# Attention of the last three batches: row sums on VectorE and a transposing DMA, in a fused attention and bilinear feed-forward kernel

## The chip, the cores and the metric

The kernel runs on one core of a Trainium2 chip. The metric is the device time of one execution in microseconds (us), and the median of several runs is compared. A core has TensorE (PE in the profile; its weight loads are PEld), VectorE (DVE), ScalarE (ACT), GpSimd (POOL) and SyncE (SP), each with its own instruction stream, and 16 DMA engines. L12 is line 12 of the kernel.

## The reference

A linear attention without softmax, normalised by the root of the mean square along each head, is followed by a feed-forward layer that multiplies two projections.

```python
# q, k, v: (batch 8, heads 8, seq 576, head_dim 64), float32
def _attn_ref(q, k, v, g_norm):
    kv = np.einsum('bhsd,bhse->bhde', k, v)
    out = np.einsum('bhsd,bhde->bhse', q, kv)
    rms = np.sqrt(np.mean(out * out, axis=-1, keepdims=True) + 1e-06)
    return (out / rms * g_norm)

# x: the attention's output as (4608 tokens, 512); w_a, w_b: (512, 1536); w_out: (1536, 512)
def _moe_ref(x, w_a, w_b, w_out):
    a = x @ w_a
    b = x @ w_b
    return (a * b @ w_out)
```

## The kernel before

**Work in two kinds.** The attention goes batch by batch (576 tokens each), the feed-forward block by block (512 tokens each, nine blocks). Both share all engines, so a batch's attention is woven between the matmuls of the blocks before the one that needs its tokens. The feed-forward takes x d-major: a column for each token, the 512 features (head pairs p = 0 to 3 of 128 features) on the partitions. These columns lie in `xp`, a ring of four batches (`R = 4 * S`), and `xcols(p, t0, n)` names n of them.

**The feed-forward.** Block 0 is plain (`std_block`, `o_std`). Blocks 1 to 8 use a Strassen form with seven products in place of eight (`wino_block` for the projections, L742; `o_unit` for the output, L911). Its sums are VectorE's work: L711 forms differences of x columns, L761 combines a PSUM bank with an evicted copy, L796 multiplies the two projections, L896 forms sums of the products, L949 combines outputs. ScalarE evicts banks (L415, L943).

**Attention of batches 2 to 7 (`late_batch`).** `load_node` has POOL issue the loads of k and v and a copy of q in bf16 to a DRAM scratch `scr`, and SP a transposing DMA that brings q d-major into `qT` (L587). Before its first load each later batch's node copies one element of the previous batch's qT to `gate_t` (L563), which makes POOL wait until that transpose has landed. `kv_mm` (L533) forms the eight 64 x 64 products, two heads to a 128 x 128 diagonal block `kvd`. Then `slices` does, for each of four head pairs and two halves of 288 tokens:

1. TensorE, L348 (`x_mm`): x = kvd times qT, d-major in PSUM;
2. ScalarE, L358 (`sq_op`): its square, in bf16;
3. TensorE, L362 (`s_mm`): a product with `ones` (blocks of 1/64), which puts a head's mean square on all of its partitions;
4. ScalarE, L366 (`rs_op`): the reciprocal root;
5. VectorE, L371 (`xt_op`): x times `g_col` times that root, to `xp` in fp16.

Batches 0 and 1 (`early_batch`) take another way to kvd and q and then the same `slices`.

**What sets the order.** `Plan` is a list scheduler that runs when the kernel is built. Every step is a node with an engine, an estimated duration, a priority (a time in us), its dependencies and the buffers that it takes and frees. `Plan.order` goes through the engines, gives each the node that can start first, the lowest priority among those ready, and emits the instructions in that order. On the chip each engine runs its stream in that order and waits on semaphores. A dependency written `(node, 8.0)` is taken by the planner as met 8.0 us after that node's end: with this it reckons with a DMA's landing. `at_win[b]` (L1025) is the window of priorities of batch b's attention, worked out from the planned starts `st` of the blocks: about 137 to 152, 171 to 184 and 206 to 216 us for batches 5, 6 and 7. The priority of the load of batch b is the window's start of batch b - 1. `RQ` and `RS` are rings of PSUM banks 5 to 7 with two held at once each, `RX` and `RY` the same over banks 0 to 3.

The estimates of durations:

```python
    def mm_us(n, cols):
        return n * (cols / 2400 + 0.0025)

    def act_us(n, bias=False):
        return (0.155 if bias else 0.06) + n / 1200

    def dve_us(n):
        return (n + 65) / 960
```

Of the kernel before, what the change touches and what calls it, by code (L numbers as in the profile page):

```python
# [8 lines left out]
FP32 = mybir.dt.float32  # L9
BF16 = mybir.dt.bfloat16  # L10
FP16 = mybir.dt.float16
AF = mybir.ActivationFunctionType  # L12
ALU = mybir.AluOpType
# [122 lines left out]
def kernel(  # L136
# [11 lines left out]
    nc = tc.nc  # L148

    B, H, S, D = q.shape  # L150
    d_model = H * D
# [30 lines left out]
    EH = d_model // 2  # L182

    const = ctx.enter_context(tc.tile_pool(name="const", bufs=1))
    scr_pool = ctx.enter_context(tc.tile_pool(name="scr", bufs=B, space=bass.MemoryType.DRAM))
    psum = ctx.enter_context(tc.tile_pool(name="psum", bufs=1, space=bass.MemoryType.PSUM))
    ctx.enter_context(tc.manual_schedule())

    def sb(name, shape, dt):
        return const.tile(shape, dt, name=name)  # L190
# [15 lines left out]
    as_t = sb("as", [128, 4, NJ, 256], FP16)  # L206
    b_ts = [sb(f"c{i}", [128, 4, 2, NMAX], FP16) for i in range(2)]
    u_t = sb("u", [128, 6, 2, NMAX], FP32)
    sq_ts = [sb(f"sq{i}", [128, HF], BF16) for i in range(3)]
    rs_ts = [sb(f"rs{i}", [128, HF], FP32) for i in range(3)]  # L210
    o_ts = [sb(f"o_sb{i}", [128, 4, d_model], FP32) for i in range(2)]

# [95 lines left out]
    def xcols(p, t0, n):  # L308
        return xp[p // 2][:, p % 2, t0 % R : t0 % R + n]
# [94 lines left out]
# [5 lines that stand above are left out]
# [7 lines left out]
        ]  # L416

    T0 = 20.0
    plan = Plan({"PE": 5.7, "DVE": 3.3, "ACT": 2.7, "SP": 5.0, "POOL": 22.5, "V": 0.0})
    PB, PA, PO = Pool(banks[0:4]), Pool(banks[5:8]), Pool(banks[4:5])  # L420
    RX, RY, RO = Ring(PB, 2), Ring(PB, 2), Ring(PO)
    RQ, RS = Ring(PA, 2), Ring(PA, 2)
    RU, RB, RAB = Ring([u_t[:, i] for i in range(6)]), Ring(b_ts), Ring(ab_ts)
    RT, RAS = Ring([T_t[:, i] for i in range(5)]), Ring([as_t[:, i] for i in range(4)])
    RSQ, RRS, ROS = Ring(sq_ts), Ring(rs_ts), Ring(o_ts)
    RK, RV, RQT, RKD = Ring(k_ts), Ring(v_ts), Ring(qT_ts), Ring(kvd)
    normed = {}
# [14 lines left out]
    def slices(at, win, extra):  # L442
        w0, w1 = win
        for i in range(2 * NP):
            p, h = divmod(i, 2)
            pr = w0 + (w1 - w0) * i / (2 * NP)
            x, s = ((Buf(RX), Buf(RY)) if at.b == 0 and i % 3 == 1 else (Buf(RQ), Buf(RS)))
            sq, rs = Buf(RSQ), Buf(RRS)
            ta = at.b * S + h * HF
            war = [  # L450
                n
                for j, (a, b) in enumerate(blocks_of)
                if a < ta - R + HF and b > ta - R
                for n in readers.get(j, ())
            ]
            n1 = plan.add(
                "PE", mm_us(1, HF), pr,
                lambda p=p, h=h, x=x: at.x_mm(p, h, x.tile), extra(p), [x], at.qt,
            )
            n2 = plan.add(  # L460
                "ACT", act_us(HF), pr, lambda p=p, h=h, b=sq: at.sq_op(p, h, b.tile), [n1], [sq]
            )
            n3 = plan.add(
                "PE", mm_us(1, HF), pr,
                lambda p=p, h=h, s=s: at.s_mm(p, h, s.tile), [n2], [s], [sq],
            )
            s_done[at.b] = n3
            n4 = plan.add(
                "ACT", act_us(HF, True), pr,
                lambda p=p, h=h, b=rs: at.rs_op(p, h, b.tile), [n3], [rs], [s],  # L470
            )
            normed[at.b, p, h] = plan.add(
                "DVE", dve_us(HF) + 0.06, pr,
                lambda p=p, h=h: at.xt_op(p, h), [n4] + war + ([g_n] if at.b == 0 else []), (), [x, rs],
            )

    def early_batch(b, win):
# [35 lines left out]
            done[p] = [n2, n4]  # L513
        slices(at, win, lambda p: done[p])

    def late_batch(b, load, win):
        at = Attn(b)
        w0, w1 = win
        kb, vb, qb = load["k"], load["v"], load["q"]
        kd = Buf(RKD)  # L520
        at.qt = [qb, kd]

        def view(t):
            return t[:, 0 : H * (NCH + 1) * D].rearrange("p (h c d) -> p h c d", h=H, d=D)

        s = Buf(RS)

        def kv_mm():
            kv_ps = s.tile[:].rearrange("p (a e) -> p a e", a=NP)
            for c in range(NCH + 1):  # L530
                for p in range(NP):
                    hs = slice(2 * p, 2 * p + 2)
                    nc.tensor.matmul(  # L533
                        kv_ps[:, p, :],
                        lhsT=kb.tile[:, c, hs, :],
                        rhs=view(vb.tile)[:, hs, c, :],
                        start=(c == 0 and p == 0),
                        stop=(c == NCH and p == NP - 1),
                    )

        n = plan.add(
            "PE", 1.15, w0, kv_mm, [(load["n"], load["kv_us"]), plan.at(w0 - 3)], [s, kd], [kb, vb]
        )

        def kv_out():
            kv_ps = s.tile[:].rearrange("p (a e) -> p a e", a=NP)
            at.kvd = kd.tile
            nc.scalar.copy(at.kvd[0:D, :, 0:D], kv_ps[0:D, :, 0:D])
            nc.scalar.copy(at.kvd[D:, :, D:], kv_ps[D:, :, D:])
            for p in range(NP):  # L550
                at.q[p] = qb.tile[:, p, :]

        m = plan.add("ACT", 0.75, w0, kv_out, [n], (), [s])
        slices(at, (w0 + 0.12 * (w1 - w0), w1), lambda p: [m, (load["qn"], 8.0)])


    def load_node(b, prio, dep):
        ld = {"k": Buf(RK), "v": Buf(RV), "q": Buf(RQT)}
        scr = scr_pool.tile([NP, S, 2, D], BF16, name="scr", tag="scr")

        def issue():
            if dep is not None:
                nc.gpsimd.tensor_copy(gate_t, dep["q"].tile[0:1, 0, 0:1])  # L563
            qv = q[b].rearrange("(p hl) s d -> hl s p d", hl=2)
            for hl in range(2):
                nc.gpsimd.dma_start(  # L566
                    out=scr[:, :, hl, :].rearrange("p s d -> s p d"), in_=qv[hl]
                )
            kt = ld["k"].tile
            ks = k[b, :, 0:SA, :].rearrange("h (sp c) d -> sp h c d", c=NCH)  # L570
            for c in range(NCH):
                nc.gpsimd.dma_start(out=kt[:, c], in_=ks[:, :, c, :])  # L572
            nc.gpsimd.dma_start(out=kt[0:SB, NCH], in_=k[b, :, SA:S, :].rearrange("h sp d -> sp h d"))
            for n, src in (("v", v),):
                t = ld[n].tile[:, 0 : H * (NCH + 1) * D].rearrange(
                    "p (h c d) -> p h c d", h=H, d=D
                )
                nc.gpsimd.dma_start(
                    out=t[:, :, 0:NCH, :],
                    in_=src[b, :, 0:SA, :].rearrange("h (sp c) d -> sp h c d", c=NCH),  # L580
                )
                nc.gpsimd.dma_start(
                    out=t[0:SB, :, NCH, :], in_=src[b, :, SA:S, :].rearrange("h sp d -> sp h d")
                )

        def transpose():
            nc.sync.dma_start_transpose(  # L587
                out=ld["q"].tile[:].rearrange("p a s -> p (a s)"),
                in_=scr[:].rearrange("a s h d -> (a s) (h d)"),
            )  # L590

        issue_us, q_us, ld["kv_us"] = (15.4, 4.3, 13.0) if dep is None else (9.0, 5.0 if b == 3 else 1.8, 13.0)

        ld["n"] = plan.add(
            "POOL", issue_us, prio, issue, [(dep["qn"], 8.0)] if dep else [], [ld["k"], ld["v"]]
        )
        ld["qn"] = plan.add(
            "SP", 2.5, prio, transpose, [(ld["n"], q_us)], [ld["q"]]
        )
        return ld  # L600
# [422 lines left out]
    for b in range(2, B):  # L1023
        t = b * S / N0
        at_win[b] = (max(53.0, st[int(t) - 1] + (t % 1) * L[int(t) - 1] - 18), st[int(t)] - 22 + (t % 1) * 12)  # L1025
    loads = {2: load_node(2, 22.5, None)}
    wo_n = load_wo(loads[2])
    for b in range(3, B):
        loads[b] = load_node(b, at_win[b - 1][0], loads[b - 1])
    gb = Buf(RQ)  # L1030
    g_in = plan.add(
        "PE", 0.07, 8.5, lambda: nc.tensor.transpose(gb.tile[:, 0:1], g_row, one), [plan.at(6.4)], [gb]
# [10 lines left out]
    for bi in range(1, nb + 1):  # L1043
        o_win = (st[bi] + 1.0, st[bi + 1] - 1.0) if bi < nb else (st[bi] + O_A, st[bi + 1] + O_B)
        if bi == 1:
            o_std(ab, muls, (o_win[0] + 4.0, o_win[1] + 4.0))
            osum = out_sums(st[2] - 10)
        else:
            o_block(bi - 1, ab, muls, osum, o_win, 2, (RO, RY, RY), 1)
        for b in needs[bi]:  # L1050
            late_batch(b, loads[b], at_win[b])
        ab, muls = wino_block(bi, (st[bi], st[bi + 1]), wsum)
    o_block(
        nb, ab, muls, osum, (st[nb + 1], st[nb + 1] + o_us[nb]), NJ // 2,
# [38 lines left out]
```

## Time and profile before

| what | value |
|---|---|
| median of 3 runs | 299.74 us (299.61 to 299.81) |
| the profiled execution | 299.53 us |
| its span, first to last instruction | 297.8 us |
| TensorE busy, share of the span | 290.5 us, 98% |
| VectorE busy | 234.0 us, 79% |
| ScalarE busy | 192.4 us, 65% |
| DMA traffic | 32.72 MB |
| first and last x of the attention written (L371) | at 10.8 and 224.6 us |

The profiled execution is one run, recorded by the hardware profiler. Its span leaves out what lies before the first and after the last instruction, here 1.7 us. A busy time is the union of the recorded durations of an engine's instructions. A matmul's record is longer than the distance to the next matmul's start, because matmuls are pipelined: a 256-column matmul is recorded with 273 ns and the next starts after 109. So TensorE's pace is read from starts.

### The profile page before, as it was taken

How to read it: one execution, taken by the hardware profiler on the slowest of the kernel's cores; microseconds unless marked ns; L12 is line 12 of the kernel's file. 1: busy time of each engine (PE TensorE's matmuls, PEld its weight loads, DVE VectorE, ACT ScalarE, POOL GpSimd, SP SyncE). 2: the span in 40 equal slices, each digit the busy share in tenths (PEclk: the TensorE clock that was granted, in tenths of full speed). 3: DMA queues.
4: the chain of work that ended last, by engine and by line, in shares of the span. 5: the costliest groups of instructions: out<-in, count | busy, mean ns of one | idle time of the engine just before them, and what ended most of it. 6: DMA issues, size and time to landing. Idle time of an engine off the chain costs nothing.

```text
span 297.8 us, 6705 instructions
## 1 busy us (share of the span) xinstructions
PE 290.5 (98%) x2635; PEld 238.9 (80%) x2635; DVE 234.0 (79%) x435; ACT 192.4 (65%) x401; POOL 76.7 (26%) x95
## 2 busy tenths in 40 slices
PE   8999999999899999999999999999999999999993
PEld 3645559865788988889888988889888888888882
DVE  5544879894976998889779977997599859897762
ACT  3847767865588577866787658954996466654521
POOL 8945830940190650380560000000000000000000
PEclk9999999999999999999999999999999999999999
DMA  8999999799999699699999200020004001100043
GB/s 178 199 199 199 194 159 155 119 166 186 202 113 172 94 191 174 42 136 210 136 146 222 74 0 2 36 108 0 2 0 143 1 2 70 73 3 0 34 144 108
DMA packets 98195, 32.72 MB, mean 110 GB/s; under 512 B 74612, under 2 KB 94068, under 8 KB 98164
## 3 DMA queue, kind: packets, MB, share of 16 engines
q0 software_dynamic: 77552, 18.44, 65.3%
q1 hardware_dynamic: 20000, 13.16, 20.3%
q10 hardware_dynamic: 612, 0.71, 0.8%
q8 instruction: 20, 0.33, 0.5%
q14 instruction: 11, 0.09, 0.1%
HBM read 37.75 MB, written 12.98 MB: 170 GB/s over the span
## 4 chain that ended last, share of the span: by engine, by line
PE 71%; DMA 22%; POOL 4%; issue 1%; DVE 1%; ACT 0%; DVEq 0%; SPq 0%; POOLq 0%
PE bk L742 42%; PE bk L911 24%; DMA scr<-in_q_dram 8%; DMA v_t<-in_v_dram 4%; DMA wb_t<-in_moe_w_b_dram 4%; DMA qT<-scr 3%; DMA wa_t<-in_moe_w_a_dram 3%; PE bk L362 2%; PE bk L348 2%; PE bk L533 2%; POOL as L237 1%; POOL so L237 1%; POOL scr L566 1%; DVE o_sb L949 1%; POOL wo_t L609 1%
## 5 line engine op out<-in xcount | busy, mean ns | idle before, releaser
L761 DVE TENSOR_TENSOR c<-bk,u 128x512 f16<-128x512 f32 x144 | 96.6, 685 | 25.2 <-ACT u L415 12.8
L415 ACT COPY u<-bk 128x512 f32<-128x512 f32 x144 | 81.8, 590 | 37.3 <-PE bk L742 33.8
L742 PE MATMUL bk<-xp,wa_t 128*128 128x256 f16 x288 | 54.9, 273 | 0.0
L742 PE MATMUL bk<-xp,wb_t 128*128 128x256 f16 x288 | 54.9, 273 | 0.0
L371 DVE SCALAR_TENSOR_TENSOR xp<-bk,g_col,rs 128x288 f16<-128x288 f32 x64 | 32.4, 511 | 14.3 <-ACT rs L366 14.3
L742 PEld LDWEIGHTS <-wa_t 128*128 128x128 f16 x384 | 37.4, 98 | 5.7
L911 PEld LDWEIGHTS <-abt 128*128 128x128 f16 x384 | 37.4, 98 | 4.7 <-DVE abt L796 0.2
L742 PEld LDWEIGHTS <-wb_t 128*128 128x128 f16 x384 | 37.6, 98 | 4.4
L415 ACT CAST c<-bk 128x512 f16<-128x512 f32 x48 | 28.1, 590 | 17.7 <-PE bk L742 16.9
L911 PE MATMUL bk<-wo_t,abt 128*128 128x256 f16 x288 | 36.8, 273 | 0.0
L742 PE MATMUL bk<-T,sb 128*128 128x256 f16 x192 | 36.6, 273 | 0.0
L742 PE MATMUL bk<-T,sa 128*128 128x256 f16 x192 | 36.6, 273 | 0.0
L366 ACT ACTIVATE rs<-bk,eps_t 128x288 f32<-128x288 f32 x64 | 32.3, 508 | 5.7 <-PE bk L362 5.2
L796 DVE TENSOR_TENSOR abt<-c 128x1024 f16<-128x1024 f16 x48 | 32.9, 686 | 1.8
L742 PEld LDWEIGHTS <-sa 128*128 128x128 f16 x288 | 28.1, 98 | 3.8
L911 PEld LDWEIGHTS <-as 128*128 128x128 f16 x288 | 28.2, 98 | 3.5
L742 PEld LDWEIGHTS <-sb 128*128 128x128 f16 x288 | 28.2, 98 | 3.3
L943 ACT COPY o_sb<-bk 128x512 f32<-128x512 f32 x31 | 18.2, 587 | 15.2 <-PE bk L911 14.8
L358 ACT ACTIVATE sq<-bk 128x288 bf16<-128x288 f32 x64 | 25.5, 414 | 1.3 <-PE bk L348 0.6
L911 PE MATMUL bk<-so,as 128*128 128x256 f16 x192 | 25.5, 273 | 0.0
L572 POOL DMA_DIRECT2D k_t<-in_k_dram x24 | 21.2, 897 | 0.7 <-issue 0.5
L566 POOL DMA_DIRECT2D scr<-in_q_dram x12 | 19.6, 1637 | 2.6 <-issue 1.4
(99 smaller groups left out, 396.5 us busy)
## 6 DMA issues: line engine op xcount, KB each, us to landing
out_dram<-o_sb SPq DMA_DIRECT2D x20, 256.0 KB, 2.3
scr<-in_q_dram POOLq DMA_DIRECT2D x12, 288.0 KB, 8.2
k_t<-in_k_dram POOLq DMA_DIRECT2D x24, 128.0 KB, 8.8
v_t<-in_v_dram POOLq DMA_DIRECT2D x6, 512.0 KB, 10.9
out_dram<-o_sb SPq DMA_DIRECT2D x18, 128.0 KB, 2.4
wa_t<-in_moe_w_a_dram POOLq DMA_DIRECT2D x6, 256.0 KB, 10.7
wb_t<-in_moe_w_b_dram POOLq DMA_DIRECT2D x6, 256.0 KB, 10.9
wo_t<-in_moe_w_out_dram POOLq DMA_DIRECT2D x2, 768.0 KB, 9.4
```

Of the source, the lines that this page charges most:

```text
L237: nc.gpsimd.dma_start(out=t[n][:, hs, :, :], in_=src[b, hs].rearrange("h (sp c) d -> sp h c d", c=EC),)
L358: nc.scalar.activation(sq, self.x_ps[p, h][:, 0:HF], AF.Square)
L366: nc.scalar.activation(rs, self.s_ps[p, h][:, 0:HF], AF.Abs_reciprocal_sqrt, bias=eps_t)
L371: nc.vector.scalar_tensor_tensor(out=xcols(p, self.b * S + h * HF, HF), in0=self.x_ps[p, h][:, 0:HF], scalar=g_col, in1=self.rs[p, h], op0 ...
L415: ("ACT", act_us(n), lambda: nc.scalar.copy(*args())),
L566: nc.gpsimd.dma_start(out=scr[:, :, hl, :].rearrange("p s d -> s p d"), in_=qv[hl])
L572: nc.gpsimd.dma_start(out=kt[:, c], in_=ks[:, :, c, :])
L742: nc.tensor.matmul(ps.tile[:, i * n : (i + 1) * n], lhsT=lhs(w, sm)[:, kc, :], rhs=rhs()[:, kc, :], start=start and i == 0 and kc == 0, st ...
L761: lambda: nc.vector.tensor_add(cs(fi, h), full(ps), u.tile),
L796: nc.vector.tensor_mul(t, c[:, :, :, 0], c[:, :, :, 1])
L911: nc.tensor.matmul(ps.tile[:, sub * EH : (sub + 1) * EH], lhsT=lhs(slice(j, j + 1))[:, 0, sub * 128 : (sub + 1) * 128], rhs=rhs[:, j, :], ...
L943: lambda: nc.scalar.copy(o(fi, h), bank(X, every)), [dep], takes, frees,
```

## The change

For batches 5, 6 and 7 (`TB = 5`) `late_batch` calls `token_tiles` in place of `slices`. It takes the batch's 576 tokens in five tiles of 128 (the last overlaps the fourth and keeps 64). For each, x comes token-major, tokens on the partitions and 512 features in the row, from four matmuls with q as the stationary operand and kvd as the moving one. ScalarE squares the whole tile, VectorE sums each head's 64 squares with a reduce, ScalarE takes eight reciprocal roots for each token, VectorE multiplies x by them into fp16, and SP stores the tile to a DRAM scratch `xs`. After the five stores SP issues four transposing DMAs (`turn`), one for each head pair, from `xs` to the columns in `xp`. VectorE then multiplies these columns by `g_col` in place, in two instructions. The planner takes the transposes as landed `TURN = 9.0` us after their node's end.

The windows of these batches start and end 13 us earlier (`AHEAD`). The load of batch 7 also waits for the turn of batch 5, by one more copy to `gate_t`. The load nodes are made just before their batch's attention instead of all at the start. The planner's estimate for the landing of batch 3's k and v goes from 13 to 16 us. There are two square buffers of 512 columns where there were three of 288.

```diff
@@
-    sq_ts = [sb(f"sq{i}", [128, HF], BF16) for i in range(3)]
+    sq_ts = [sb(f"sq{i}", [128, d_model], BF16) for i in range(2)]
+    ss_t = sb("ss", [128, 3, 2 * H], FP32)
+    xt_t = sb("xt", [128, 2, d_model], FP16)
@@
+    TB, TURN, AHEAD = 5, 9.0, 13.0
@@
+    RSS, RXT = Ring([ss_t[:, i] for i in range(3)]), Ring([xt_t[:, i] for i in range(2)])
@@
+    def token_tiles(at, win, dep):
+        b = at.b
+        w0, w1 = win
+        xs = xscr_pool.tile([NP, S, 128], FP16, name="xs", tag="xs")
+        stored, tiles = [], [(i * 128, 128) for i in range(NCH)] + [(S - 128, SB)]
+        for i, (j0, keep) in enumerate(tiles):
+            pr = w0 + (w1 - w0) * i / len(tiles)
+            X, sq, ss, xt = Buf(RQ), Buf(RSQ), Buf(RSS), Buf(RXT)
+
+            def mm(j0=j0, X=X):
+                for p in range(NP):
+                    nc.tensor.matmul(
+                        X.tile[:, p * 128 : (p + 1) * 128],
+                        lhsT=at.q[p][:, j0 : j0 + 128],
+                        rhs=at.kvd[:, p, :],
...
+            n1 = plan.add("PE", 0.23, pr, mm, dep, [X], at.qt)
+            n2 = plan.add(
+                "ACT", act_us(d_model), pr,
+                lambda X=X, sq=sq: nc.scalar.activation(sq.tile, X.tile[:], AF.Square), [n1], [sq],
+            )
+            n3 = plan.add(
+                "DVE", dve_us(d_model), pr,
+                lambda sq=sq, ss=ss, heads=heads: nc.vector.tensor_reduce(
+                    out=ss.tile[:, 0:H], in_=heads(sq.tile), axis=mybir.AxisListType.X, op=ALU.add
+                ),
+                [n2], [ss], [sq],
+            )
+            n4 = plan.add(
+                "ACT", act_us(H, True), pr,
+                lambda ss=ss: nc.scalar.activation(
+                    ss.tile[:, H:], ss.tile[:, 0:H], AF.Abs_reciprocal_sqrt, bias=eps_t, scale=1.0 / D
+                ),
+                [n3],
+            )
+            n5 = plan.add(
+                "DVE", dve_us(d_model), pr,
+                lambda X=X, ss=ss, xt=xt, heads=heads: nc.vector.tensor_mul(
+                    heads(xt.tile), heads(X.tile[:]), ss.tile[:, H:].unsqueeze(2).to_broadcast([128, H, D])
+                ),
+                [n4], [xt], [X, ss],
+            )
+
+            def save(j0=j0, keep=keep, xt=xt):
+                nc.sync.dma_start(
+                    out=xs[:, j0 + 128 - keep : j0 + 128, :].rearrange("a s e -> s a e"),
+                    in_=xt.tile[128 - keep :].rearrange("p (a e) -> p a e", a=NP),
+                )
+
+            stored.append(plan.add("SP", 0.45, pr, save, [n5], (), [xt]))
...
+        def turn():
+            for p in range(NP):
+                nc.sync.dma_start_transpose(out=xcols(p, b * S, S), in_=xs[p])
+
+        n6 = plan.add("SP", 2.5, w1, turn, stored + war)
+        for i in range(2):
+            xg = xp[i][:, :, b * S % R : b * S % R + S]
+            n7 = plan.add(
+                "DVE", 0.4, w1, lambda xg=xg: nc.vector.tensor_scalar_mul(xg, xg, g_col), [(n6, TURN)]
+            )
...
+        if b >= TB:
+            return token_tiles(at, (w0 + 0.12 * (w1 - w0), w1), [m, (load["qn"], 8.0)])
         slices(at, (w0 + 0.12 * (w1 - w0), w1), lambda p: [m, (load["qn"], 8.0)])
@@ load_node
+            if xt is not None:
+                nc.gpsimd.tensor_copy(gate_t, xcols(NP - 1, (b - 2) * S, 1)[0:1])
...
-        issue_us, q_us, ld["kv_us"] = (15.4, 4.3, 13.0) if dep is None else (9.0, 5.0 if b == 3 else 1.8, 13.0)
+        issue_us, q_us, ld["kv_us"] = (15.4, 4.3, 13.0) if dep is None else (9.0, 5.0 if b == 3 else 1.8, 16.0 if b == 3 else 13.0)
...
-            "POOL", issue_us, prio, issue, [(dep["qn"], 8.0)] if dep else [], [ld["k"], ld["v"]]
+            "POOL", issue_us, prio, issue, ([(dep["qn"], 8.0)] if dep else []) + ([(xt, TURN)] if xt else []), [ld["k"], ld["v"]]
@@
+        if b >= TB:
+            at_win[b] = tuple(x - AHEAD for x in at_win[b])
@@
-            late_batch(b, loads[b], at_win[b])
+            if b > 2:
+                loads[b] = load_node(b, at_win[b - 1][0], loads[b - 1], turned.get(b - 2))
+            turned[b] = late_batch(b, loads[b], at_win[b])
```

More of the change, by code (lines that the diff above doesn't have):

```diff
@@ L184 @@
     const = ctx.enter_context(tc.tile_pool(name="const", bufs=1))
+    xscr_pool = ctx.enter_context(tc.tile_pool(name="xscr", bufs=B, space=bass.MemoryType.DRAM))
     scr_pool = ctx.enter_context(tc.tile_pool(name="scr", bufs=B, space=bass.MemoryType.DRAM))
@@ L460, in slices @@
             n2 = plan.add(
-                "ACT", act_us(HF), pr, lambda p=p, h=h, b=sq: at.sq_op(p, h, b.tile), [n1], [sq]
+                "ACT", act_us(HF), pr, lambda p=p, h=h, b=sq: at.sq_op(p, h, b.tile[:, 0:HF]), [n1], [sq]
             )
@@ L514, in early_batch, with heads @@
         slices(at, win, lambda p: done[p])
+    def token_tiles(at, win, dep):
[12 more added lines that the diff above has]
+                        rhs=at.kvd[:, p, :],
+                        start=(p == 0),
+                        stop=(p == NP - 1),
+                        skip_group_check=True,
+                    )
+            def heads(ap):
+                return ap.rearrange("p (h d) -> p h d", d=D)
+            n1 = plan.add("PE", 0.23, pr, mm, dep, [X], at.qt)
[30 more added lines that the diff above has]
+            stored.append(plan.add("SP", 0.45, pr, save, [n5], (), [xt]))
+        war = [
+            n
+            for j, (u, v) in enumerate(blocks_of)
+            if u < (b + 1) * S - R and v > b * S - R
+            for n in readers.get(j, ())
+        ]
+        def turn():
[6 more added lines that the diff above has]
+                "DVE", 0.4, w1, lambda xg=xg: nc.vector.tensor_scalar_mul(xg, xg, g_col), [(n6, TURN)]
+            )
+            for p in (2 * i, 2 * i + 1):
+                for h in range(2):
+                    normed[b, p, h] = n7
+        return n6
@@ L553, in late_batch, with load_node @@
         m = plan.add("ACT", 0.75, w0, kv_out, [n], (), [s])
+        if b >= TB:
+            return token_tiles(at, (w0 + 0.12 * (w1 - w0), w1), [m, (load["qn"], 8.0)])
         slices(at, (w0 + 0.12 * (w1 - w0), w1), lambda p: [m, (load["qn"], 8.0)])
-    def load_node(b, prio, dep):
+    def load_node(b, prio, dep, xt=None):
         ld = {"k": Buf(RK), "v": Buf(RV), "q": Buf(RQT)}
@@ L1025 @@
         at_win[b] = (max(53.0, st[int(t) - 1] + (t % 1) * L[int(t) - 1] - 18), st[int(t)] - 22 + (t % 1) * 12)
+        if b >= TB:
+            at_win[b] = tuple(x - AHEAD for x in at_win[b])
     loads = {2: load_node(2, 22.5, None)}
     wo_n = load_wo(loads[2])
-    for b in range(3, B):
-        loads[b] = load_node(b, at_win[b - 1][0], loads[b - 1])
+    turned = {}
     gb = Buf(RQ)
```

## The prediction

> **What bounds the kernel now.** I read the busy table first, then the groups by line, then TensorE's timeline, because a busy share of TensorE is modelled and can hide small gaps.
>
> ```profile
> span 297.8 us, 6705 instructions
> PE 290.5 (98%) x2635; PEld 238.9 (80%) x2635; DVE 234.0 (79%) x435; ACT 192.4 (65%) x401; POOL 76.7 (26%) x95
> ```
>
> The reader is to see one engine near the whole span, and VectorE (DVE) next at 79%. The timeline of TensorE (start, duration, instruction) around two of the six k-times-v products tells whether TensorE is really full:
>
> ```profile
> 76.90 1.06 PE L533 MATMUL bk<-v_t,k_t 128*128 128x128 bf16 x16
> 79.15 0.38 PE L533 MATMUL bk<-v_t,k_t 128*128 128x128 bf16 x4 [1.19 <-DMA v_t<-in_v_dram]
> ```
> ```profile
> 138.57 1.28 PE L533 MATMUL bk<-v_t,k_t 128*128 128x128 bf16 x20
> 139.69 0.38 PE L742 MATMUL bk<-xp,wa_t 128*128 128x256 f16 x2
> ```
>
> In the second pair twenty matmuls of 128 columns take 139.69 - 138.57 = 1.12 us from start to the next start: 56 ns each. Matmuls of 256 columns start every 109 ns (the chain has twelve in 1.31 us), and those of 288 every 122 ns: all are columns / 2.4 plus 2.5 ns. I compared every start-to-start distance from 45 to 293 us with that rule: the excess sums to 1.50 us, and 1.35 us of it is the one gap in the first pair, where batch 3's product waits for v. So from 45 us on TensorE is the bound, with no other wait; only its columns, that gap, and new waits can move the end.
>
> The groups that the change touches (busy sum, mean ns), all with 64 instructions, eight for each batch:
>
> ```profile
> L371 DVE SCALAR_TENSOR_TENSOR xp<-bk,g_col,rs 128x288 f16<-128x288 f32 x64 | 32.4, 511 | 14.3 <-ACT rs L366 14.3
> L366 ACT ACTIVATE rs<-bk,eps_t 128x288 f32<-128x288 f32 x64 | 32.3, 508 | 5.7 <-PE bk L362 5.2
> L358 ACT ACTIVATE sq<-bk 128x288 bf16<-128x288 f32 x64 | 25.5, 414 | 1.3 <-PE bk L348 0.6
> ```
>
> and the stretches of one feed-forward block each in which batches 5 to 7 fall (PE, PEld, DVE, ACT, POOL busy):
>
> ```profile
> 105.30:135.80 30.50, 30.50 (x280) 27.12 (x278) 26.90 (x49) 22.16 (x45) 12.41 (x15) 1.00 1.58 141
> 135.80:166.30 30.50, 30.50 (x289) 27.25 (x288) 26.15 (x48) 21.96 (x46) 9.21 (x10) 1.00 1.39 167
> 166.30:196.80 30.50, 30.50 (x289) 27.21 (x288) 25.67 (x48) 21.74 (x46) 0.00 (x0) 1.00 0.11 34
> 196.80:227.30 30.50, 30.50 (x289) 27.23 (x288) 25.21 (x47) 21.74 (x46) 0.00 (x0) 1.00 0.10 30
> ```
>
> VectorE has 3.6 to 5.3 us free of each 30.5; ScalarE (ACT) 8.3 or more.
>
> **What the Trainium skill says.** "TensorE: Matmul & The Clock Gate", section "Back-to-back issue gap", gives a sustained 81 ns for a 128-column matmul with its own weights, and 56 ns for an isolated one. The trace has 56 ns over twenty in a row, each with a new weight load, so I take 56 and keep 81 as a bound. "VectorE: DVE Perf Modes", section "The perf-mode tier table", has tensor_reduce at one element a cycle whatever the type, and tensor_scalar on 16-bit SBUF data at four. No row of before shows either. "DMA: Bandwidth & Descriptors", section "Two DMAs through the same engine are not ordered", says that completion order isn't kept in one queue, so the turning transposes must wait for the stores' landing; the q path already shows such a wait (SP on scr, 68.0 us in five waits).
>
> **TensorE, part by part.** For one batch the change removes 8 products with kvd and 8 with ones, 288 columns each: 16 x 0.1225 = 1.96 us. It adds 5 tiles of 4 matmuls of 128 columns: 20 x 0.056 = 1.12 us. Net -0.84 us, three batches -2.52 us; at 81 ns a matmul it would be -0.34 and -1.0. The longer load estimate of batch 3 (16 instead of 13 us) lets the planner place its k-times-v product up to 3 us later, after v has landed at 79.1, with other matmuls in front. I count the whole 1.35 us; the lower end is nothing, if no other matmul is ready then.
>
> **ScalarE.** Removed for a batch: 8 x (0.414 + 0.508) = 7.4 us. Added: 5 squares of 512 elements (the 512-element copy of L415 is 0.590) and 5 reciprocal roots of 8 elements (the one-element warm-up took 0.203), about 4.0 us. It gains 3.4 us, hidden under TensorE: worth nothing by itself.
>
> **VectorE.** Removed: 8 x 0.511 = 4.1 us. Added: 5 reduces of 512 and 5 products of 512 from PSUM, both at L761's 0.685 (one element a cycle as well), 6.9 us, and two multiplications by g over 1152 fp16 elements. At four a cycle 0.46 each, estimated from that page's 693 ns for 2048; at two, from L796's 686 ns for 1024, 0.75. I take 0.46, so 7.8 us against 4.1: +3.7 us a batch, +11.1 in all (+12.8 at most). The four stretches hold 103.9 us; 115.0 must fit in 122.0 - 2.5 = 119.5. That is 96%. It fits, but not in place: each batch's tiles are planned 13 us earlier, into 124 to 139, 158 to 171 and 193 to 203 us, where VectorE already had 89%, 95% and 94%. Taking the old x operations out (0.5 us in each of the first two) and 6.9 us in, 19.8, 18.7 and 16.7 us stand in windows of 15, 13 and 10.4: an overflow of 4.8, 5.7 and 6.3 us. Behind each window is room: 142 to 158 had 12.4 us busy of 16, of which 3.6 were the old x operations. What slides is not late: block 5 first needs batch 5 in VectorE's differences at about 160 (L711 starts at 158.55), TensorE at 166. VectorE ran without a gap from 105 to 118 while TensorE lost nothing, so short saturation is covered by the ready matmuls. I charge 0.2 us a batch, 0.6 us in all; lower end nothing.
>
> **SP, POOL and DMA.** SP gains 5 stores and 4 transposes a batch. A store costs SP some 0.8 us to issue (eight output stores took 6.45), the four transposes together as much as the one q transpose of equal bytes, 5.5 to 6.5 us; it has 10 us more in each 30, and queued behind are output stores, whose two buffers are reused two blocks (61 us) later, and the next q transpose, needed 20 us later. Nothing on the path. POOL's last load now waits for batch 5's turn: it started at 144.6 and will start near 155; it took 20 us, so it lands at 175 and is needed at 193. The new wait that matters is VectorE's: the multiplication by g waits for the turn, and everything behind it on VectorE is held. Planned from the last product: 2.8 us to the store's landing, 2.5 for issue, 9.0 for landing, together 14.3. Measured: output stores land after 2.3 to 6.1 us (medians of their four sizes), q transposes 7.5 to 11.9 us from issue (median 9.9): 10 to 18, typically 14. So this costs nothing typically; at worst it holds VectorE for 4 us. Third square buffer gone: the early slices take turns with the root on ScalarE, so two suffice; nothing, at most 0.3 us.
>
> **Sum.** The profiled execution took 299.53 us (span 297.8 and 1.7 around it). 299.53 - 2.52 - 1.35 + 0.6 = 296.3. The median of the runs is 0.2 higher than the profiled one, so 296.5.
>
> **Rivals.**
> *Weights bind.* If 128-column matmuls run at 81 ns, the saving is 1.0, not 2.5: 298.0. For it speaks only the page; against it the 56 ns. Chance 0.06.
> *VectorE gives it all back.* The gain of 3.9 us is eaten by combinations (L761) queued behind reduces, so that TensorE waits for a PSUM bank: about 1.1 us a batch: 299.7. Chance 0.08.
> *VectorE becomes the bound in the windows.* The three overflows are 16.8 us in all. If a third of them can't slide because the planner lets tile work with older priorities go first, TensorE loses 5.6 us: 299.7 - 3.9 + 5.6 = 301.4. It decides for slower once more than 3.9 + 0.6 = 4.5 us of the 16.8 reach TensorE. For it: the planner counts a 512-element operation as 0.60 us where the trace has 0.685, so it sees room that is not there. Against it: the same error stands in the kernel now, at 86%, without a gap. Chance 0.22.
> *The turn lands late.* 4 us late on VectorE less the 1.9 us that VectorE waits today (longest wait of L761 for ScalarE) without TensorE stopping, is 2.1, three times 6.3 us: 299.7 - 3.9 + 6.3 = 302.1. Against it: at that time no load runs beside the turn, since the last load is gated. Chance 0.08.
>
> **How the numbers follow.** The forecast has 0.56. Faster by more than 0.2% (0.6 us, about what a measurement of this kernel can tell from no change): 0.56 + 0.06 = 0.62. Within it 0.08, slower 0.30. The range runs from 295.6 (no stall at all is 295.9, less 0.3 for what two runs differ) to 301.8, past the third rival's point; the likeliest case alone is 295.7 to 298.5.
>
> **What would show it.** TensorE's busy sum falls by about 2.5 us; start-to-start distances in the new tiles are 56 ns; the gap at 79 us is gone; the reduce takes about 0.69 and the g multiplication 0.46 us; VectorE is above 93% from 124 to 224 us. Wrong would be: TensorE waits on L761 or on a token product (rivals two and three), a VectorE wait of over 2 us on the transposing DMA (rival four), or 80 ns spacing (rival one).

## The result, and the profile after

The changed kernel takes 306.94 us in the median (305.81 to 307.15, four runs) against 299.68 before: a ratio of 1.0234, 95% interval 1.0209 to 1.0259. The forecast was 296.5, with a range up to 301.8. The change made the kernel slower by 7.3 us, and by a mechanism that the prediction had put down as costing nothing. Of the runs below, one execution of b_kv16 took 780.42 us and is left out.

The page of the changed kernel: span, busy times, and from the 40 slices TensorE's busy tenths and its granted clock (7.6 us a slice):

```profile
span 304.8 us, 6759 instructions
PE 290.6 (95%) x2646; PEld 238.7 (78%) x2648; DVE 243.6 (80%) x447; ACT 186.4 (61%) x383; POOL 77.7 (25%) x96
...
PE   8999999999999999994799999999999999999993
...
PEclk9999999999999999998699999999999999999998
```

The reader is to see one hole, in the slices from 137 to 152 us, and a lower clock in it. Everywhere else TensorE's tenths are as before. TensorE's busy sum has not fallen although it has fewer columns: its slow stretch adds 1.4 us of busy time, and since a matmul's record is longer than the distance to the next start, the records reach into the gaps. The timelines of TensorE, VectorE and SP through the hole (start, duration, instruction, and in brackets the idle time before it and its releaser):

```profile
140.18 0.38 PE L830 MATMUL bk<-T,sb 128*128 128x256 f16 x2
146.50 0.59 PE L830 MATMUL bk<-xp,sa 128*128 128x256 f16 x2 [5.94 <-DVE c L849]
```
```profile
138.17 0.68 DVE L849 TENSOR_TENSOR c<-bk,u 128x512 f16<-128x512 f32 x1
145.16 0.69 DVE L565 TENSOR_TENSOR xt<-bk,ss 128x512 f16<-128x512 f32 x1 [6.30 <-DMA xs<-xt]
145.76 0.68 DVE L849 TENSOR_TENSOR c<-bk,u 128x512 f16<-128x512 f32 x1
```
```profile
133.08 6.69 SPq L675 DMA_TRANSPOSE qT<-scr  x1
139.87 2.21 SPq L572 DMA_DIRECT2D xs<-xt  x2
```

Read from the bottom. (Lines have moved: L675 is the q transpose of L587 before, L849 the combination of L761, L830 the product of L742.) SP begins the q transpose of batch 6 at 133.08 and can issue nothing else until 139.77. Behind it in SP's stream stand the stores of batch 5's first two token tiles, finished by VectorE at 133.0 and 135.9. They are issued at 139.87, and the first lands at 145.06. There are two `xt` tiles, so the third token product (L565) may not write until then: VectorE stands still for 6.30 us. The next combination (L849) stands behind it in VectorE's stream, and TensorE needs that one's PSUM bank: 5.94 us idle. Afterwards TensorE runs at half pace for 2.9 us, as the windows' clock column shows (0.50):

```profile
146.40:149.30 2.90, 2.80 (x14) 1.99 (x14) 2.90 (x7) 0.93 (x3) 0.00 (x0) 0.50 0.20 51
```

**Where the 7.41 us went.** Profiled executions: 299.53 before, 306.94 after. From TensorE's starts, with columns / 2.4 plus 2.5 ns for each matmul's due share and the rest as excess (fillers are matmuls at the start whose results nothing reads):

| term | before | after | difference |
|---|---|---|---|
| from the span's start to the first matmul | 1.19 | 1.19 | 0 |
| due share of the real matmuls | 280.31 | 277.78 | -2.53 |
| excess from 46 us to the end | 1.50 | 10.08 | +8.58 |
| start-up: fillers and excess before 46 us | 9.78 | 10.50 | +0.72 |
| from the last matmul's start to the span's end | 4.96 | 5.25 | +0.29 |
| outside the span | 1.78 | 2.13 | +0.35 |

Of the 10.08 us, the stop is 6.10 and the half pace after it 1.39. Ten smaller gaps make up 2.54 us.

### The profile page after: what moved, and what is told of

Read it like the earlier page. It is cut to its first block, busy times and chain, and to the rows that moved or that the text cites. A ratio compares the mean times of both kernels' runs of the same rounds, so it can differ in the third digit from the quotient of the medians.

```text
span 304.8 us, 6759 instructions
## 1 busy us (share of the span) xinstructions
PE 290.6 (95%) x2646; PEld 238.7 (78%) x2648; DVE 243.6 (80%) x447; ACT 186.4 (61%) x383; POOL 77.7 (25%) x96
## 4 chain that ended last, share of the span: by engine, by line
PE 68%; DVE 11%; DMA 11%; issue 3%; POOL 2%; SPq 2%; ACT 0%; DVEq 0%; POOLq 0%
PE bk L830 35%; PE bk L999 19%; PE bk L385 7%; DVE c L849 4%; DMA qT<-scr 4%; PE bk L934 3%; DMA wb_t<-in_moe_w_b_dram 3%; DMA scr<-in_q_dram 3%; SPq L675 2%; DMA xs<-xt 2%; POOL as L240 1%; DVE abt L884 1%; PE bk L617 1%; PE bk L365 1%; PE bk L351 1%
## 5 line engine op out<-in xcount | busy, mean ns | idle before, releaser
L849 DVE TENSOR_TENSOR c<-bk,u 128x512 f16<-128x512 f32 x144 | 96.7, 686 | 20.1 <-PE bk L830 14.2
L830 PE MATMUL bk<-xp,wa_t 128*128 128x256 f16 x288 | 55.4, 274 | 0.2
L830 PE MATMUL bk<-xp,wb_t 128*128 128x256 f16 x288 | 55.2, 274 | 0.0
L830 PEld LDWEIGHTS <-wa_t 128*128 128x128 f16 x384 | 37.5, 99 | 6.7 <-issue 1.1
L830 PEld LDWEIGHTS <-wb_t 128*128 128x128 f16 x384 | 37.8, 98 | 4.7
L830 PE MATMUL bk<-T,sb 128*128 128x256 f16 x192 | 36.7, 273 | 0.0
L830 PE MATMUL bk<-T,sa 128*128 128x256 f16 x192 | 36.6, 272 | 0.0
L830 PEld LDWEIGHTS <-sa 128*128 128x128 f16 x288 | 27.9, 98 | 10.7 <-issue 7.1
L830 PEld LDWEIGHTS <-sb 128*128 128x128 f16 x288 | 28.2, 98 | 3.4
L999 PEld LDWEIGHTS <-as 128*128 128x128 f16 x288 | 28.2, 98 | 3.3
L374 DVE SCALAR_TENSOR_TENSOR xp<-bk,g_col,rs 128x288 f16<-128x288 f32 x40 | 20.3, 513 | 11.2 <-ACT rs L369 11.2
L830 PE MATMUL bk<-xp,sa 128*128 128x256 f16 x96 | 18.5, 275 | 6.6 <-DVE c L849 6.5
L369 ACT ACTIVATE rs<-bk,eps_t 128x288 f32<-128x288 f32 x40 | 20.0, 506 | 6.6 <-PE bk L365 6.4
```

Source lines behind the costliest of these rows:

```text
L369: nc.scalar.activation(rs, self.s_ps[p, h][:, 0:HF], AF.Abs_reciprocal_sqrt, bias=eps_t)
L374: nc.vector.scalar_tensor_tensor(out=xcols(p, self.b * S + h * HF, HF), in0=self.x_ps[p, h][:, 0:HF], scalar=g_col, in1=self.rs[p, h], op0 ...
L830: nc.tensor.matmul(ps.tile[:, i * n : (i + 1) * n], lhsT=lhs(w, sm)[:, kc, :], rhs=rhs()[:, kc, :], start=start and i == 0 and kc == 0, st ...
L849: lambda: nc.vector.tensor_add(cs(fi, h), full(ps), u.tile),
L999: nc.tensor.matmul(ps.tile[:, sub * EH : (sub + 1) * EH], lhsT=lhs(slice(j, j + 1))[:, 0, sub * 128 : (sub + 1) * 128], rhs=rhs[:, j, :], ...
```

## The experiments

The theory that I took from the profile (A): the stores' place behind the q transpose, together with a ring of two, stops VectorE, and VectorE stops TensorE. The main rival (B) was the prediction's own: VectorE simply has too much work there. Each edit below is against the changed kernel unless it says otherwise.

**xt5: five tiles instead of two.** No engine's order changes.

```diff
-    xt_t = sb("xt", [128, 2, d_model], FP16)
+    xt_t = sb("xt", [128, 5, d_model], FP16)
-    ... RXT = ... Ring([xt_t[:, i] for i in range(2)])
+    ... RXT = ... Ring([xt_t[:, i] for i in range(5)])
```

> The changed kernel with five xt tiles in place of two; each engine's order of instructions stays as it is, only the wait of VectorE's token product for an xt tile goes. Theory A (the stores of the token tiles sit behind the q transpose on SP, VectorE waits 6.3 us for an xt tile and TensorE stops behind it, then runs at half pace for some 3 us): 6.1 + 1.5 us go, 306.9 becomes 299.3, and between 138 and 150 us TensorE has no gap over 0.5 us. Rival B (VectorE has too much work there, and the wait only hides the backlog): the backlog reaches TensorE in another place, 303 or more.

Measured 298.91 us, 0.9973 of the kernel before (0.9958 to 0.9988). The excess after 46 us fell from 10.08 to 2.33 us. VectorE's timeline of xt5 where the 6.30 us had been:

```profile
137.47 0.68 DVE L849 TENSOR_TENSOR c<-bk,u 128x512 f16<-128x512 f32 x1
138.07 0.68 DVE L565 TENSOR_TENSOR xt<-bk,ss 128x512 f16<-128x512 f32 x1
138.67 0.68 DVE L849 TENSOR_TENSOR c<-bk,u 128x512 f16<-128x512 f32 x1
```

The product follows without a wait, and the stores are as late as before (SP is again busy with the q transpose until 139.34). So A holds and B falls as the main cause: with the same work in the same order VectorE keeps up, except for some 2 us.

**xt3: three tiles.** The same edit with 3.

> The changed kernel with three xt tiles in place of two (five in xt5); orders as they are. If the ring of xt tiles is what ties VectorE to the late stores, the third token product no longer waits and the fourth, due at 141.4 us as in xt5, waits for the first store: issued at 139.4 behind the q transpose and landed by about 144.0, so some 2.6 us, of which TensorE's slack covers a part: 300 to 302, between xt5 (298.9) and the changed kernel (306.9). If depth alone mattered in no such way, it equals one of the two.

Measured 303.01 us, 1.0100 (1.0068 to 1.0132). The fourth product waits:

```profile
144.86 0.69 DVE L565 TENSOR_TENSOR xt<-bk,ss 128x512 f16<-128x512 f32 x1 [3.21 <-DMA xs<-xt]
```

The wait moved by one tile, as expected. The time missed the expected range by 1.0 us: VectorE waited 3.21 us where some 2.6 were expected, little of it was covered (TensorE stopped for 2.66 us), and then TensorE ran 15 matmuls at half pace (1.6 us), which I had not expected.

**no_kv6 and no_qt6: what makes SP and the stores late.** One leaves out the loads of k and v of batch 6, the other its q transpose; TensorE, VectorE and ScalarE keep their order.

```diff
+            if b == 6: return                       # no_kv6, in issue(), after the loads of q
             kt = ld["k"].tile
...
-            nc.sync.dma_start_transpose(
+            b != 6 and nc.sync.dma_start_transpose( # no_qt6, in transpose()
```

> The changed kernel (two xt tiles) without the loads of k and v for batch 6 (its attention then uses what batch 4 left); orders on TensorE, VectorE, ScalarE and SP as they are. Theory F (load 6's k and v keep the DMA engines busy from 127 to 143 us, the q transpose on SP takes 6.7 us to issue and 11 to land for that reason, and the stores behind it land late): the q transpose issues faster, the stores land 2 us after issue, and VectorE's wait of 6.3 us at 138 falls to under 3; 300 to 303. Theory G (the q transpose alone holds SP and the engines that long): the wait stays at 5 us or more, 305 to 307.

> The changed kernel (two xt tiles) without the q transpose of batch 6 (its attention then uses the q that batch 4 left); orders as they are but for SP, which has one transpose less. Theory G: VectorE's wait at 138 us goes entirely, 299 to 299.7. Theory F alone: stores are no longer behind the transpose on SP, but still land after 5 to 9 us while the loads run; the first two are issued at 133 and 136, so that the wait falls to 1 to 4 us: 300 to 303.

no_kv6 took 299.78 us, 1.0012 (1.0001 to 1.0023), and no_qt6 302.19, 1.0082 (1.0069 to 1.0095). SP in no_kv6:

```profile
132.51 2.24 SPq L675 DMA_TRANSPOSE qT<-scr  x1
134.85 1.08 SPq L572 DMA_DIRECT2D xs<-xt  x2
```

Without the loads beside it the same transpose is issued in 2.24 us in place of 6.69, the second store lands 2.56 us after its issue, and VectorE's wait at 138 us is gone (0.4 us remain at 176, in batch 6). The time lies 0.2 us under theory F's range. Without the transpose but with the loads, the stores are issued at 132.55 and 135.40, and the first still needs until 140.74 to land: 8.2 us. VectorE waits for it:

```profile
140.83 0.69 DVE L565 TENSOR_TENSOR xt<-bk,ss 128x512 f16<-128x512 f32 x1 [2.47 <-ACT u L418]
```

The releaser named here is a ScalarE copy with which the product has nothing to do; it ended at about the same time. The instruction waits on two semaphores, and the store's reached its last step at 140.74. So theory F holds: the loads of batch 6's k and v are behind both halves of the delay. The wait for SP behind the transpose adds 3.8 us to VectorE's wait (6.30 against 2.47).

**save_act: the stores issued by ScalarE.** (Two tiles.)

```diff
-                nc.sync.dma_start(
+                nc.scalar.dma_start(
                     out=xs[:, j0 + 128 - keep : j0 + 128, :].rearrange("a s e -> s a e"),
...
-            stored.append(plan.add("SP", 0.45, pr, save, [n5], (), [xt]))
+            stored.append(plan.add("ACT", 0.1, pr, save, [(n5, 0.18)], (), [xt]))
...
-        n6 = plan.add("SP", 2.5, w1, turn, stored + war)
+        n6 = plan.add("SP", 2.5, w1, turn, [(s, 2.6) for s in stored] + war)
```

The last line tells the planner when to count the stores as landed. The whole edit changes the order on every engine but POOL.

> The changed kernel (two xt tiles), with the stores of the token tiles issued by ScalarE in place of SP. Theory A: the stores no longer queue behind the q transpose, VectorE's wait for an xt tile falls under 1 us, 298.5 to 300.5. Rival C (the stores' packets are held behind the transpose's on the 16 DMA engines, whoever issues them): the stores land after 5 us as now and some 3 us of the stop remain, 302 to 304.

Measured 307.74 us, 1.0259 (1.0213 to 1.0306): no gain, and outside the ranges of both theories. The stores' landing between 125 and 150 us, and who waited (from the waits):

```profile
DMA to landing us min/median/max: 2.0/4.0/9.3
```
```profile
DVE xt L565 <- DMA xs<-xt: 5.8, 2, 3.5
ACT c L418 <- DVE xt L565: 4.3, 1, 4.3
```

Issued at 132.15 and 135.00, free of SP's queue, the stores land 9 us later at the worst. VectorE's wait at 138 falls only from 6.3 to 3.5 us, a second one comes with batch 6, and the third store now holds ScalarE for 4.3 us, since its issue waits for the delayed product. So SP's queue alone is not the cause; of the two, rival C has the first stop right, with the loads (no_kv6) in the place of the transpose. "DMA: Bandwidth & Descriptors", section "Issuing engines are not separate DMA queues", says that DMAs of all issuers run on the same 16 engines and interleave. This run agrees: beside the loads the stores took up to 9.3 us from ScalarE, and 8.2 from SP (no_qt6).

**sp65: the planner told of SP's real time.**

```diff
-            "SP", 2.5, prio, transpose, [(ld["n"], q_us)], [ld["q"]]
+            "SP", 6.5 if b >= TB else 2.5, prio, transpose, [(ld["n"], q_us)], [ld["q"]]
```

> The changed kernel (two xt tiles), with the planner's estimate of SP's time for the q transposes of batches 5 to 7 raised from 2.5 to 6.5 us; nothing else. Theory A (SP is held 6.7 us by the q transpose where the planner reckons with 2.5): the planner puts other work of VectorE ahead of the token product that waits, and most of the 7.6 us go: 299 to 302. Rival C (what holds the store is not SP's issue but the DMA rings, so that the estimate for SP doesn't matter): the stop at 140 us stays, 305 to 307.

Measured 307.54 us, 1.0265 (1.0243 to 1.0286). The total fits C, but its place does not. The stop at 140 us fell from 6.10 to 1.65 us, as A had it, since the first two stores now go ahead of the transpose. A new stop of 5.35 us stands at 176 us. VectorE waits there for batch 6's first store, which was issued at 169.53, ahead of the q transpose of batch 7, and took 8.84 us to land beside load 7:

```profile
178.46 0.69 DVE L565 TENSOR_TENSOR xt<-bk,ss 128x512 f16<-128x512 f32 x1 [4.62 <-DMA xs<-xt]
```

The second store is queued behind that transpose, which held SP for 8.84 us as well, and brings a shorter wait. One better estimate for SP moved the collision to the next batch; it does nothing about the slow landing.

**b_kv16 and b_sq2: two side effects alone, in the kernel before.**

```diff
-  ... (9.0, 5.0 if b == 3 else 1.8, 13.0)
+  ... (9.0, 5.0 if b == 3 else 1.8, 16.0 if b == 3 else 13.0)     # b_kv16
-    sq_ts = [sb(f"sq{i}", [128, HF], BF16) for i in range(3)]
+    sq_ts = [sb(f"sq{i}", [128, HF], BF16) for i in range(2)]      # b_sq2
```

> The kernel before with batch 3's landing estimate at 16 instead of 13 us, nothing else. If the gap of 1.35 us at 79 us goes and no other comes, 299.7 becomes 298.3. Rival: at 79 us no other matmul is ready and the gap only changes its place, 299.7.

> The kernel before with two square buffers of 288 columns in place of three. If the missing buffer costs in the start-up, block 0 begins 0.6 us later, 300.3. Rival: two suffice, 299.7.

b_kv16: 298.30 us (three executions), 0.9957 (0.9940 to 0.9973). The gap of 1.35 us is gone and one of 0.26 stands at 80 us. b_sq2: 299.41 us, 0.9986 (0.9975 to 0.9998), no loss; in its profile the start-up is 0.6 us longer and the gap at 79 us 0.5 us shorter, and the first of these varies between runs as much.

**xt5_sq3: five tiles and three square buffers.**

> As xt5, and with three square buffers in place of two. If the third buffer's loss cost 0.64 us in the first 46 us (TensorE's start-to-start distances there), this is 0.6 us under xt5, 298.7. Rival: those 0.64 us came from the first k and v landing later in that one execution, then it equals xt5; as the planner's whole order changes with the ring, other gaps can move it by up to 1 us either way.

298.19 us, 0.9956 (0.9940 to 0.9973). The interval overlaps that of xt5. Whether the third square buffer is worth up to 0.7 us or nothing stays open. With it the token-major way is as fast as b_kv16, which has none of it: 298.2 and 298.3. The 2.5 us fewer columns have been given back.

**Who gives them back: red8, g_act, est** (on xt5_sq3). red8 shortens VectorE's reduce, g_act moves the multiplication by g to ScalarE, and est gives the planner the lengths of the traced records of the token tile's steps (its lines are shortened here).

```diff
-  out=ss.tile[:, 0:H], in_=heads(sq.tile), ...
+  out=ss.tile[:, 0:H], in_=heads(sq.tile)[:, :, 0:8], ...                    # red8
-  "DVE", 0.4, w1, lambda xg=xg: nc.vector.tensor_scalar_mul(xg, xg, g_col), ...
+  "ACT", 1.2, w1, lambda xg=xg: nc.scalar.activation(xg, xg, AF.Copy, scale=g_col), ...   # g_act
-  square act_us(d_model), reduce dve_us(d_model), root act_us(H, True), product dve_us(d_model)
+  square 0.60, reduce 0.66, root 0.31, product 0.66                          # est
```

> Five xt tiles, three square buffers, and a reduce that adds only 8 of each head's 64 squares (the row sums are left incomplete); every engine's order is that of xt5_sq3. VectorE has some 0.45 us less in each of 15 tiles, 6.8 us in all. Theory D (of TensorE's 2.5 us fewer columns some 2 us come back as short waits for VectorE in the windows of the tiles): the excess of 2.3 us in TensorE's starts falls to 0.3 to 1.0, 296.4 to 297.1. Rival E (those waits come from the planner's order or from ScalarE, not from VectorE's load): it stays at 298.2.

> Five xt tiles, three square buffers, and the multiplication by g on ScalarE in place of VectorE. Theory D: VectorE is freed of 0.95 us a batch, a quarter to a half of the 2 us come back, 297.2 to 297.8. Rival E: no gain, 298.2; and if ScalarE, held by its wait for the turn, delays evictions, 299.

> Five xt tiles, three square buffers, and the planner's durations of the token tile's steps set to what the trace of the changed kernel shows in a row of such instructions (square 0.60, reduce and product 0.66, root 0.31 us, in place of 0.49, 0.60, 0.60 and 0.16). Theory H (the 2 us that come back on TensorE come from steps that take longer than the planner reckons): the excess in TensorE's starts falls from 2.3 to about 1, 297.0. Rival: the planner's order changes as a whole and other gaps take the place, 298.2 or up to 299.

red8 took 297.56 us, 0.9930 (0.9918 to 0.9942), its excess after 46 us falling from 2.33 to 1.69. g_act took 298.78, 0.9975 (0.9965 to 0.9985), no gain, with new gaps from 224 to 231 us. est took 297.34, 0.9935 (0.9916 to 0.9955), with an excess of 1.50. So by these traces, one execution each, VectorE's load is about a third of it: 6.8 us less work on VectorE brought 0.6 us. est brought as much without taking away any work. But it did not set wrong durations right. Its numbers are lengths of records, and in a row, without gaps, the steps start every 0.49 us (square), 0.59 (reduce), 0.60 (product) and 0.20 (root), against 0.49, 0.60, 0.60 and 0.16 in the planner before. What est adds is mostly a margin, and the order on TensorE, VectorE and ScalarE changes with it. That this order brings the gain, and which part of it, isn't shown. VectorE in est is as busy as ever (PE, PEld, DVE, ACT, POOL in two stretches):

```profile
135.00:165.00 30.00, 30.00 (x296) 27.09 (x295) 28.22 (x51) 19.33 (x39) 7.96 (x9) 1.00 0.89 137
165.00:195.00 30.00, 30.00 (x294) 26.96 (x292) 27.33 (x49) 19.38 (x40) 1.68 (x3) 1.00 1.13 157
```

At 28.2 of 30 us on VectorE, TensorE is full. est has the lowest median of all; two of its six executions took 298.8 and 298.9 us, and its interval overlaps those of red8, xt5_sq3 and b_kv16.

## Why the prediction was wrong

**TensorE's columns: right.** Predicted -2.52 us at 56 ns a matmul, measured -2.53; twenty token matmuls a batch run at that pace. The rival "Weights bind" falls.

**The gap at 79 us: right, a little too large.** 1.35 us was counted; a gap of 0.27 came in its place. In the timeline of after, the product (L617) runs in one piece, and the gap follows behind other matmuls at 81.15:

```profile
79.81 1.28 PE L617 MATMUL bk<-v_t,k_t 128*128 128x128 bf16 x20
80.93 0.38 PE L830 MATMUL bk<-T,wa_t 128*128 128x256 f16 x2
81.15 0.38 PE L830 MATMUL bk<-T,wb_t 128*128 128x256 f16 x2
81.64 1.47 PE L999 MATMUL bk<-wo_t,abt 128*128 128x256 f16 x12
```

**SP: this step failed.** "... queued behind are output stores ... and the next q transpose ... Nothing on the path." It asked what stands behind the new work on SP, and not what the new work stands behind. The q transpose was in the profile of before, inside the window into which batch 5's tiles were planned:

```profile
130.65 0.91 SPq L814 DMA_DIRECT2D out_dram<-o_sb  x2
133.61 6.39 SPq L587 DMA_TRANSPOSE qT<-scr  x1
```

The two output stores, issued at 130.65 and 131.06, landed after 6.0 and 6.6 us. The step also counted the ring of output tiles and overlooked the ring of two `xt` tiles, the one that VectorE waits for. The cost was 7.5 us where zero stood: 6.1 of stop and 1.4 of half pace, for which the prediction has no term. The fourth rival had the same mechanism, a late DMA that holds VectorE, but at the wrong DMA, and with 1.9 us of cover before TensorE stops. The runs show hardly any cover: waits of 6.30, 3.21 and 2.47 us on VectorE (after, xt3, no_qt6) became stops of 6.10, 2.66 and 2.28 on TensorE.

**The turn: right in direction.** Nothing waits for it on VectorE. The four transposes of batch 5 took 6.5 us from first issue to last landing (155.12 to 161.61), less than the 7.5 to 11.9 that a q transpose had taken. Its gate has a price that the prediction did not see: load 7 ran from 145.05 to 161.21 us before, and now runs from 162.25 to 179.66, beside the stores of batch 6's tiles, the first of which took 5.16 us to land. In that stretch the second stops of sp65 and save_act arise.

**VectorE's durations: right as records, too long as a pace; its effect: too small.** The groups of the changed kernel (busy sum, mean ns, idle before):

```profile
L565 DVE TENSOR_TENSOR xt<-bk,ss 128x512 f16<-128x512 f32 x15 | 10.3, 685 | 6.5 <-DMA xs<-xt 6.3 <-ACT ss L558 0.2
L551 DVE TENSOR_REDUCE ss<-sq 128x8 f32<-128x512 bf16 x15 | 10.2, 677 | 0.0
L593 DVE TENSOR_SCALAR xp<-xp,g_col 128x1152 f16<-128x1152 f16 x6 | 3.7, 651 | 0.0
```

The reduce takes 677 ns (0.685 taken). The g multiplication (0.46 taken) takes 513 to 516 in batches 6 and 7, and 892 and 954 in batch 5, for a reason that stays open. VectorE's busy sum rose by 9.6 us; 11.1 was predicted. That sum added up lengths of records, but neighbouring records overlap: in xt5's timeline above records of 0.68 us start 0.60 apart, and before, 102 combinations (L761) with the next instruction right behind them took 0.601 in the median. So for steps in a row the planner's 0.60 us was right, the third rival's argument that it "sees room that is not there" falls, and the overflows were reckoned too high. Even so the effect was larger than forecast. I charged 0.6 us for short stalls, and xt5 shows 2.33 less the 0.26 that b_kv16 has too: 2.1 us. This term is 1.5 us short. red8 puts about a third of it on VectorE's load, est, with another order, had 0.8 us less of it, and the rest stays open. ScalarE, set at "worth nothing by itself", may be in it, since its root waits for the reduce and evictions stand behind it. In the waits of the changed kernel:

```profile
ACT ss L558 <- DVE ss L551: 7.9, 3, 6.1
```

Of these 7.9 us, 6.1 belong to the stop at 140 us. In xt5 1.7 remain, and whether they reach TensorE isn't shown.

**Not foreseen and not explained:** 0.3 us more after the last matmul, which the other token-major kernels with stores on SP show too, and 0.35 outside the span. The start-up term of +0.72 us varies between executions of one order (xt5 has 9.80 us there with two square buffers, after 10.50) and isn't put down to the change. The corrected sum with the measured terms: 299.53 - 2.53 - 1.08 + 7.5 + 2.2 + 0.7 + 0.3 + 0.35 = 307.0.

## What to carry to other kernels

When a step joins a queue, list what is already in front of it in that queue at that time, with durations from the trace, and follow its buffers to the engine that refills them: a ring of two turned a late store into a stop of VectorE and TensorE. A store's landing is to be priced from the stretch in which it will run: here 2 us in a quiet one and 5 to 9 beside a load. A stop has a second price, the half pace behind it, here 1.4 us. Don't add up the lengths of records for an engine that works in a row; take the distance from start to start. When a removed bound gives nothing back, look at the short waits that return and at the order; here another order lowered the median by 0.85 us, within overlapping intervals.

## What the runs showed of the hardware

- A transpose of 0.59 MB held SP for 2.24 us with the batch's k and v loads left out and for 6.69 with them. Issuing a DMA is not a fixed cost.
- TensorE drops to half pace (1.2 GHz by the spacing: 213 ns from start to start in place of 109 for a 256-column matmul) after stops of 2.66, 3.02, 3.37, 5.35 and 6.10 us and not after 1.65 or 2.28, and stays there for 2.9 to 5.1 us. "TensorE: Matmul & The Clock Gate", section "What's actually happening", gives one idle window of about 3.4 us as the condition; xt3's stop of 2.66 us was enough. In the traces' records of the granted clock, every stretch between two changes is a multiple of 3.413 us long. Counted in such windows from the first rise of the clock, half clock followed each window at full clock in which TensorE stood idle for 2.16 us or more (five cases, in four kernels), and none with 1.93 or less; the 2.28 us of no_qt6 lay across two windows. So where a stop falls counts as well as its length. No run was made to test this.
